# Pacing the Toeplitz loads of the middle chunks in a planned attention-plus-S4 kernel

## The chip, the cores and the metric

The kernel runs on one core of one Trainium2 chip. The metric is the device time of one execution in microseconds (us). A core has five engines that run their own instruction lists side by side and meet only at semaphores: TensorE (PE, matmuls; PEld is its weight load), VectorE (DVE), ScalarE (ACT), GpSimd (POOL) and SyncE (SP, which here only issues DMAs). Matmuls write to PSUM, eight banks of 128 x 512 f32; everything else lies in SBUF or in DRAM. Within one engine's list instructions start in order, so an instruction that waits holds up all that stand behind it on that engine.

## The reference

The output is a gated mix of two branches over a sequence of 2048 tokens with 448 channels, all in bf16:

```python
g = sigmoid((x * gate_w).sum(-1))
a = attention(x)      # 16 query heads of 28, one key and one value head
b = s4(x)             # y = causal convolution of x with K, + x * Dskip
out = g * a + (1 - g) * b
```

The attention is `softmax(q k^T / sqrt(28)) v`, then a 448 x 448 output matrix. The convolution kernel is K[d, l] = Re sum over 256 states n of C[d,n] dB[d,n] exp(l dt[d] A[d,n]); the reference multiplies spectra, which is a causal convolution of length 2048 for each channel.

## The kernel before

**Attention.** Scores are made transposed, in tiles of 128 keys x 512 queries for one head; there are 1024 such tiles. They are taken in turns of three and two, which gives 410 "score sets". For each set PE makes the scores into `psS` (L1318, L1341), ACT takes their exponential into `expT` (L1373), and PE multiplies them with the values into `psB` (L1392). Five PSUM banks hold scores, so the scores of set n (sets are numbered from 0 here) can start when the exponential of set n-2 has read its banks.

**The S4 branch.** The 448 channels go in 14 chunks of 32. For each chunk DVE builds tables of powers (`tables`, L954 to L1004), PE makes the 32 kernels K from them (`kgen`, L1027), DVE copies them to `kstg` (L1039), and POOL writes them to DRAM (`KP_scratch`). From there they come back as Toeplitz matrices: `tload` reads, for each of 8 channels, 128 rows, each the same sequence shifted by one element, into one of the buffers of `T` (three until late in the kernel). One load is four DMAs of 272 KB on SP's queue; 56 loads cover all channels. `conv` then multiplies each Toeplitz block with the input held in `U` (PE, L1094), DVE multiplies the result by 1-g (L1104), PE turns it back (L1115) and DVE adds it to `O` (L1124). `ufill` is another group of DMAs on SP's queue (`U<-T`), which refills `U` for the second half of the channels.

**What sets the order.** Nothing is ordered by hand. Each operation is recorded with an estimated duration, a priority and what it depends on; `Prog.schedule` then plays the engines through in planned time, at each step taking the operation that can start earliest (`key = (r, o.pr, i)`), and writes one list for each engine. The times of this plan exist only while the kernel is built. What is left of them is the order of each list, and the waits that `waits` makes from the dependencies: a wait that an earlier one on the same engine implies is left out. Three things in it matter here.

- A T load takes its turn on SP when its kernels are in DRAM and the last convolution that read its buffer is done.
- After a load the planned time at which its convolution may start is later than the load's planned end by a margin: 56 ns, and `LATE` = 1000 ns more for loads planned before 300000 ns.
- PE's instructions are counted in blocks of 256 (`BLOCK`), and PE may not enter a block in the plan before a set time (`FETCH`) after it entered the one before. Where PE has nothing to do the plan puts in a matmul that has no use (`filler`, L1300).

The first operations of SP's, PE's, DVE's and POOL's lists that a change in the plan moves are thus followed by others: every later choice can fall otherwise. ACT's list has one order.

Of the kernel before, what the change touches and what calls it, by code (L numbers as in the profile page):

```python
# [91 lines left out]
class Prog:  # L92
# [5 lines left out]
    SWITCH = 105.0  # L98
    BLOCK, FIRST, FETCH, IDLE, NEED, QUIET = 256, 158, 4800.0, 3300.0, 0.015, 480000.0
    HALF = (0.0, 0.0, 1.0)  # L100
    PORT = 0.55
    POOL = (7, 5)
    SLACK = {"pe": 500.0, "dve": 300.0}
# [76 lines left out]
    def schedule(self):  # L180
        ops = self.ops
# [17 lines left out]
        order = {e: [] for e in ENG}  # L199
# [5 lines left out]
        npe = 0  # L205
        block = [0.0, 0.0]
        opened = False
        past = []
        self.tot = {}
        self.clock = {e: {} for e in ENG}  # L210
# [4 lines left out]
        while done < n:  # L215
            best = None
            for e in ENG:
                T = free[e]
                for i in ready[e]:
                    o = ops[i]  # L220
                    r = max(rt[i], T)
                    if o.lock is not None:
                        L = min((x for x in locks if x[0] is None), key=lambda x: x[1], default=None)
                        if L is None:
                            continue
                        r = max(r, L[1] + (300.0 if o.pr >= 2 else 0.0))
                    for k in o.comm or ():
                        if k in comm:
                            r = max(r, ops[comm[k]].end)
                    if e == "pe":  # L230
                        j = (npe + o.ni - self.FIRST - 1) // self.BLOCK + 1
                        if j < len(block):
                            r = max(r, block[j])
                            if o.pr >= 1 and block[-1] > r:
                                left = self.FIRST + (len(block) - 2) * self.BLOCK - npe - o.ni
                                r = max(r, block[-1] - left / self.NEED)
                    key = (r, o.pr, i)
                    if best is None or key < best[0]:
                        best = (key, e, i)
            assert best is not None, "scheduler stuck"  # L240
            (r, _, _), e, i = best
            o = ops[i]
            spare = [x for x in locks if x[0] is None and x[1] <= free[e]]
            if e == "pe" and (opened or spare) and r > self.FWIN and self.filler is not None and npe > self.FIRST + self.BLOCK:
                T = free[e]
# [4 lines left out]
                if r - T >= w and busy < self.FLOW * self.FWIN and (j >= len(block) or block[j] <= T):  # L250
                    b = 6 if opened else spare[0][3]
                    o = self.op("pe", lambda x, b=b: self.filler(x, b), self.FILL, rd=["one", "id"], ni=2)
# [7 lines left out]
                    i, r = o.i, T  # L260
                    ready[e].append(i)
            ready[e].remove(i)
            if e == "pe" and o.mode != mode:
                r = max(r, free[e] + self.SWITCH)
# [4 lines left out]
            if e == "pool" and o.slot is None:  # L269
                for d in reversed(order[e]):  # L270
                    if ops[d].slot is None:
                        o.deps[d] = 1
                        break
            order[e].append(i)
            for k in o.comm or ():
                if k in comm:
# [19 lines left out]
            else:  # L296
                ns = o.ns
                if e == "pe" and self.HALF[0] < r < self.HALF[1]:
                    ns *= self.HALF[2]
                free[e] = r + ns  # L300
                end = free[e] + o.lat
                if e == "pool" and o.ns >= 500.0:
                    free["dve"] = max(free["dve"], r) + self.PORT * o.ns
            o.end = end
# [4 lines left out]
            for j in succ[i]:  # L309
                need[j] -= 1  # L310
                x = ops[j]
                if i not in x.deps:
                    t = free[e]
                elif x.eng == e and o.slot is None and e == "pe":
                    t = free[e]
                elif x.eng == e and o.slot is None:
                    t = free[e] + self.SAME[e]
                else:
                    t = end + self.SEM_NS
                    if x.eng == "pe" and x.pr in self.LAZY:  # L320
                        t += self.LAZY[x.pr] if o.slot is None else self.LATE if o.slot[0] == "T" and r < 300000.0 else 0.0
                    if x.pr == 1.45:
                        t += self.FAR
                    elif x.pr >= 2 or x.pr == 1.5:
                        t += self.SLACK.get(x.eng, 0.0)
                rt[j] = max(rt[j], t)
                if need[j] == 0:
                    ready[x.eng].append(j)
# [1159 lines left out]
```

## Time and profile before

| | us |
|---|---|
| median of 3 runs | 499.83 (499.33 to 502.65) |
| the profiled execution, whole | 499.53 |
| its span, first to last instruction | 497.8 |
| ACT busy | 484.2 |
| of it exponentials, 410 of them | 464.5 |
| PE busy | 476.5 |
| DVE busy | 455.1 |
| T loads: median from issue of one DMA to landing | 4.9 |

The profile is one execution. Its page gives busy times of each engine; a chain, which is followed back from the last instruction to what released it; groups of instructions by line; and the DMA issues. L1318 is line 1318 of the kernel before. "PE psS L1094 <- DMA T<-KP_scratch" means that PE stood idle until that DMA landed, and "issue" means that the engine waited for nothing that the profile names. The granted TensorE clock was 1.00 up to 488 us of the span and 0.99 in the rest.

### The profile page before, as it was taken

What the parts mean: (1) busy time and instruction counts of PE and PEld (TensorE: products, weight loads), DVE (VectorE), ACT (ScalarE), POOL (GpSimd) and SP (SyncE); (2) the same over time, 40 slices, a digit from 0 to 9 for tenths busy, and PEclk for the clock granted to TensorE, in tenths of its full rate; (3) what the DMA queues carried; (4) which work ended last, traced back from release to release, by engine and by line L of the source; (5) the groups of instructions that cost most, each with busy time, mean ns of one, the idle gap of its engine ahead of it and who ended that gap; (6) DMA issues with size and microseconds to landing.
All of it is one profiled execution on the core that took longest, in us unless ns stands there. A gap on an engine that the chain in (4) does not pass through costs nothing.

```text
span 497.8 us, 17345 instructions
## 1 busy us (share of the span) xinstructions
PE 476.5 (96%) x7641; PEld 208.2 (42%) x7641; DVE 455.1 (91%) x867; ACT 484.2 (97%) x436; POOL 146.2 (29%) x282
## 2 busy tenths in 40 slices
PE   8899999999999999899999999999999999999997
PEld 6432233343443444444344344444444344344553
DVE  6999999999999999999999999998999999995313
ACT  6999999999999999999999999999999999999995
POOL 2102044234143433224306044520612524251110
PEclk9999999999999999999999999999999999999999
DMA  8997696928529556893953962689793596759742
GB/s 266 324 173 185 118 157 133 261 74 250 152 49 284 166 155 126 247 246 57 288 129 51 285 156 77 184 244 290 176 283 39 144 314 185 212 135 302 234 160 70
DMA packets 152423, 91.86 MB, mean 185 GB/s; under 512 B 84538, under 2 KB 148332, under 8 KB 152348
## 3 DMA queue, kind: packets, MB, share of 16 engines
q1 hardware_dynamic: 143370, 81.21, 61.4%
q0 software_dynamic: 8704, 9.41, 7.6%
q8 instruction: 60, 0.98, 0.8%
q10 hardware_dynamic: 274, 0.14, 0.1%
q14 instruction: 15, 0.12, 0.1%
HBM read 73.61 MB, written 5.23 MB: 158 GB/s over the span
## 4 chain that ended last, share of the span: by engine, by line
ACT 86%; PE 7%; DMA 2%; issue 0%; SPq 0%
ACT expT L1373 85%; DMA T<-KP_scratch 2%; PE psS L1341 1%; PE psS L1318 1%; PE psB L1392 1%; PE psB L1294 1%; PE psS L1231 1%; PE psX L1094 0%; PE psS L1094 0%; SPq L158 0%; PE psB L1300 0%; PE psS L1027 0%; PE psS L873 0%; PE psB L1386 0%; PE psX L1027 0%
## 5 line engine op out<-in xcount | busy, mean ns | idle before, releaser
L1373 ACT ACTIVATE expT<-psS 128x1536 bf16<-128x1536 f32 (+1 forms) x410 | 464.5, 1410 | 2.5 <-PE psS L1341 1.5
L968 DVE TENSOR_TENSOR tab<-tab,mbf 128x512 bf16<-128x512 bf16 (+4 forms) x140 | 139.7, 1002 | 0.0
L1318 PE MATMUL psS<-qT,kT 29*128 29x512 bf16 x684 | 95.7, 385 | 10.7 <-ACT expT L1373 5.5
L1392 PE MATMUL psB<-expT,vaug 128*32 128x512 bf16 x1000 | 99.9, 390 | 0.1
L1341 PE MATMUL psS<-qM,kT 128*128 128x512 bf16 x316 | 95.1, 384 | 1.2 <-ACT expT L1373 0.5
L158 POOL DMA_DIRECT2D KP_scratch<-kstg x104 | 57.4, 559 | 78.1 <-DVE kstg L1039 74.8
L983 DVE TENSOR_TENSOR tab<-tab 128x256 bf16<-128x256 bf16 (+4 forms) x140 | 77.3, 576 | 0.0
L1392 PEld LDWEIGHTS psB<-expT,vaug 128*32 128x32 bf16 x1000 | 25.6, 93 | 73.3 <-issue 70.5
L158 POOL DMA_DIRECT2D qM<-qT x64 | 32.4, 514 | 62.9 <-DVE qT L885 33.0
L1318 PEld LDWEIGHTS psS<-qT,kT 29*128 29x128 bf16 x684 | 23.7, 91 | 64.3 <-ACT expT L1373 51.8
L1300 PE MATMUL psB<-ident,one 128*128 128x512 bf16 x148 | 48.2, 384 | 0.0
L158 POOL DMA_DIRECT2D rdenB<-R_scratch x60 | 31.0, 523 | 48.8 <-DMA R_scratch<-denT 48.7
L1094 PE MATMUL psX<-T,U 128*26 128x128 bf16 (+3 forms) x1728 | 38.6, 221 | 1.2 <-issue 1.0
L1094 PE MATMUL psS<-T,U 128*26 128x128 bf16 (+3 forms) x1536 | 35.6, 221 | 1.1 <-DMA T<-KP_scratch 1.1
L1094 PEld LDWEIGHTS psX<-T,U 128*26 128x26 bf16 (+3 forms) x1728 | 29.6, 105 | 15.0 <-issue 10.0
L158 POOL DMA_DIRECT2D denT<-acc x15 | 10.7, 711 | 85.6 <-DVE acc L1153 72.6
L1094 PEld LDWEIGHTS psS<-T,U 128*26 128x26 bf16 (+3 forms) x1536 | 27.3, 105 | 13.3 <-issue 7.6
L997 DVE TENSOR_TENSOR tab<-tab,tmp 128x1984 bf16<-128x1984 bf16 x28 | 32.4, 1184 | 0.0
L1341 PEld LDWEIGHTS psS<-qM,kT 128*128 128x128 bf16 x316 | 19.0, 97 | 28.5 <-ACT expT L1373 19.5
L991 DVE TENSOR_TENSOR tmp<-tmp,mq 128x64 bf16<-128x64 bf16 (+4 forms) x70 | 25.4, 363 | 0.0
L914 DVE TENSOR_TENSOR msq<-seedz 128x512 f32<-128x512 f32 (+1 forms) x40 | 24.7, 618 | 0.0
L1300 PEld LDWEIGHTS psB<-ident,one 128*128 128x128 bf16 x148 | 13.3, 97 | 22.1 <-issue 14.4
(186 smaller groups left out, 491.2 us busy)
## 6 DMA issues: line engine op xcount, KB each, us to landing
T<-KP_scratch SPq DMA_DIRECT2D x204, 272.0 KB, 4.9
U<-KP_scratch SPq DMA_DIRECT2D x20, 272.0 KB, 5.5
rdenB<-R_scratch POOLq DMA_DIRECT2D x60, 64.0 KB, 4.1
U<-cst SPq DMA_DIRECT2D x1, 3584.0 KB, 25.0
qM<-qT POOLq DMA_DIRECT2D x64, 32.0 KB, 3.3
tab<-in_A_x_dram SPq DMA_DIRECT2D x4, 448.0 KB, 4.7
O<-in_A_x_dram SPq DMA_DIRECT2D x16, 112.0 KB, 4.8
O<-cst SPq DMA_DIRECT2D x1, 1792.0 KB, 9.6
```

The costliest lines, as they stand in the source:

```text
L158: return [e.dma_start(o, i, **kw) for o, i in pairs]
L914: pg.op("dve", lambda e: e.tensor_tensor(m2(msq), z2, z2, ALU.mult), el(2 * n), rd=[kr, ki] + first, wr=["msq"], pr=pr)
L968: mul = lambda e, o, a, b: e.tensor_tensor(o, a, b, ALU.mult)
L983: vo(lambda e, dv=dv, tv=tv, k=k: e.tensor_tensor(dv, dv, tv, ALU.add if k else ALU.subtract), n, [kt[k], kd[k]], [kd[k]], 1.92 if lv else ...
L991: vo(lambda e, w=w, lv=lv: e.tensor_tensor(rho.v(0, P, (32 - 2 * w) * 2, [[64, 32], [2, w], [1, 2]]), rho.v(0, P, (32 - w) * 2, [[64, 32], ...
L997: vo(lambda e, k=k: e.tensor_tensor(tab.v(0, P, FM + k * FP + 2, [[64, 32], [2, 31], [1, 2]]), tab.v(0, P, lm + k * PL + 62, [[64, 32], [- ...
L1094: r = e.matmul(ps.v(32 * j, 32 - m0, 128 * k, [[1, 128]]), self.U.v(0, P, (4 * gi + j) % UA // 2 * 128 + 2 * (2 * m0 + par) + j % 2, [[4, ...
L1300: return e.matmul(t.v(0, P, off, [[1, 512]]), self.one.v(0, P, 2, [[0, P]]), self.ident.v(0, P, 0, [[0, 4], [1, P]]), start=b != 6, stop=b ...
L1318: r = e.matmul(self.psS.v(0, P, 512 * b, [[1, 512]]), kT.v(32 * h, DH + 1, 128 * kt, [[1, 128]]), qT.v(32 * h, DH + 1, 512 * (i % 2), [[1, ...
L1341: return e.matmul(self.psS.v(0, P, 512 * b, [[1, 512]]), kT.v(0, P, 128 * kt, [[1, 128]]), self.qM.v(0, P, (i % 2) * XQ + 512 * h, [[1, 51 ...
L1373: o = pg.op("act", lambda e: e.activation(expT.v(0, P, 512 * es[0], spread(es, n)), self.psS.v(0, P, 512 * bs[0], spread(bs, n)), AF.Exp, ...
L1392: r = e.matmul(self.psB.v(32 * h, 32, 0, [[1, 512]]), vaug.v(0, P, 32 * kt, [[1, 32]]), expT.v(0, P, 512 * ring[t], [[1, 512]]), start=(kt ...
```

## The change

Three edits of the planner, and nothing else. While a T load would start in planned time between 195 and 360 us, it may start no earlier than 5500 ns after the T load before it. For such a load the last exponential that ended by then in the plan becomes a dependency, so the built load waits for ACT's count. And the margin `LATE` of 1000 ns applies to loads that are planned before 360 us instead of 300 us.

```diff
+    GAP, spaced = 5500.0, (195000.0, 360000.0)
...
+        lastT = 0.0
...
+                    if o.slot is not None and o.slot[0] == "T" and self.spaced[0] < r < self.spaced[1]:
+                        r = max(r, lastT + self.GAP)
                     key = (r, o.pr, i)
...
+            if o.slot is not None and o.slot[0] == "T":
+                if self.spaced[0] < r < self.spaced[1]:
+                    for d in reversed(order["act"]):
+                        if ops[d].end <= r:
+                            o.deps[d] = 1
+                            break
+                lastT = r
             order[e].append(i)
...
-                        t += self.LAZY[x.pr] if o.slot is None else self.LATE if o.slot[0] == "T" and r < 300000.0 else 0.0
+                        t += self.LAZY[x.pr] if o.slot is None else self.LATE if o.slot[0] == "T" and r < 360000.0 else 0.0
```

In the built lists ACT's order is unchanged. PE's list is the same up to its 891st of 2364 planned operations (2366 after), DVE's up to the 403rd of 867, POOL's up to the 62nd of 107 and SP's up to the 53rd of 142. Of the 56 T loads, counted from 0, the 22 from 16 to 37 now wait for a score set: for the end of the exponentials of sets 154, 159, 165, 171, 183, 189, 194, 200, 211, 217, 223, 228, 234, 247, 254, 261, 266, 271, 277, 283, 288 and 293. Two fillers are added.

## The prediction

> **What bounds the kernel now.** I read the page's busy times first, then busy times by stretch, then the waits and the chain inside the stretch that the change touches.
>
> ```profile
> PE 476.5 (96%) x7641; PEld 208.2 (42%) x7641; DVE 455.1 (91%) x867; ACT 484.2 (97%) x436; POOL 146.2 (29%) x282
> ```
>
> ACT is the bound: 464.5 us of its 484.2 are the 410 exponentials, so one score set costs 464.5 / 410 = 1.133 us, and no edit here touches an exponential. What can be won is ACT's idle time. By stretch (the columns are the stretch, its length, and the busy us and counts of PE, PEld, DVE, ACT, POOL, then clock, DMA share and GB/s):
>
> ```profile
> 0.00:20.00 20.00, 16.57 (x191) 11.33 (x192) 15.48 (x33) 14.91 (x19) 3.26 (x19) 1.00 0.96 293
> 20.00:195.00 175.00, 169.33 (x2185) 66.36 (x2181) 173.69 (x346) 174.21 (x157) 53.76 (x97) 1.00 0.70 169
> 195.00:360.00 165.00, 158.97 (x2818) 69.85 (x2810) 161.50 (x307) 163.29 (x146) 54.92 (x102) 1.00 0.71 183
> 360.00:455.00 95.00, 92.66 (x1600) 40.64 (x1601) 93.09 (x161) 95.00 (x86) 31.08 (x58) 1.00 0.70 200
> 488.00:497.80 9.80, 6.93 (x87) 3.36 (x87) 3.06 (x8) 3.82 (x5) 0.00 (x0) 0.99 0.33 89
> ```
>
> From 195 to 360 us ACT is idle for 165.00 - 163.29 = 1.71 us; before that for 0.79 from 20 us on, after it until 488 for nothing. The rest of its 13.6 idle us lies in the first 20 us and the last 9.8, which the edits do not reach. So 1.71 us is the most that the middle can give. DVE is nearly as full there: 3.50 us idle of 165, 1.91 of the next 95. The chain from 195 to 360 us (start, length, what) shows where the 1.71 are:
>
> ```profile
> 194.19 13.57 ACT expT L1373 x12
> ...
> 208.20 0.34 PE psX L1094 x15
> 208.55 0.96 issue
> 209.51 0.49 PE psX L1094 x21
> ...
> 211.80 114.46 ACT expT L1373 x101
> ...
> 331.86 7.70 DMA T<-KP_scratch
> 339.56 0.04 issue
> 339.60 0.25 PE psS L1094 x4
> ...
> 341.89 18.19 ACT expT L1373 x16
> ```
>
> There are two stalls. At 208.55 PE stands 0.96 us in the middle of a convolution, on nothing that the profile names; ACT then loses 0.56 us at 210.58 and 0.20 at 211.80. Near 339 PE waits for load 32; the waits put its size and ACT's loss as follows (total us, times, longest):
>
> ```profile
> PE psS L1094 <- DMA T<-KP_scratch: 1.1, 1, 1.1
> PE psX L1094 <- issue: 1.0, 1, 1.0
> ACT expT L1373 <- PE psS L1341: 1.3, 2, 0.7
> ```
>
> ACT's three idle gaps there (0.08 at 336.28, 0.75 at 340.74, 0.13 at 341.89) make 0.96.
>
> **The late load.** In the trace loads 29 to 34 were issued at 313.7, 319.1, 324.2, 329.9, 333.2 and 336.8. Where the records have all four landings, a load took 6.4 to 9.6 us from its first issue to its last landing: 6.4 for load 15, with nothing near it, 9.0 and 9.3 for loads 30 and 33. Load 32 had until its convolution 8.6 us or so (329.9 to 338.5, where PE went idle) and needed 9.7. In the new order it waits for the end of set 266 and its convolution stands behind the scores of set 277, which start when set 275 ends: 9 sets, 9 x 1.133 = 10.2 us, and some 0.4 for those scores. Counted likewise, loads 16 to 37 get 7 to 23 sets; only loads 30 and 36 get 7 (7.9 + 0.4 = 8.3 us), eight get 8 (9.5 us). That is above what a load takes with little beside it (6.4 to 7.9), and below the worst (9.6). I take it that this stall goes: **-0.96**. From both sides: 0 if spaced loads still take 9.6, -0.96 if not; nearest is load 15.
>
> **The stall at 208.55 stays.** PE's list is unchanged up to its 891st operation, and the stall lies in operations 879 to 887. Loads 16 and 17 now also wait for sets 154 and 159, which ended at 201.0 and 206.4; they were issued at 200.8 and 205.7 because PE then freed their buffers. So they move by 0.2 and 0.7 us. What PE waits for: the records of the DMA queue for instructions (q8 on the page: 60 transfers of 16 KB for 2 x 7641 PE instructions, about 255 in each) show one that began at 207.03 and ended at 208.18; PE went on 1.33 us later. By the count of PE's instructions the block in front of it began at 204.0. The transfer began when load 16's last packets did (207.2). The next one began at 212.51, when load 17's last packets did. With no T load under way such transfers began within 0.8 us of their block. So a code block waits behind a T load under way, whether or not another follows. Worth of this edit at this place: 0, and the next block, due at 214.97 with its transfer done at 213.46, could be up to 0.5 late now that load 17 comes 0.7 later.
>
> [...]
>
> **The added waits.** 22 waits on SP, each at the head of four DMAs. Behind each stand the rest of that load, the next loads, and pieces of the refill of `U`. The refill pieces are wanted much later: the first were issued at 185.2 and read from 320.1 on, the last at 378.8 and from 470.5 on. The next load is meant to wait. SP has the time: one DMA issue takes 0.6 us (median 615 ns), so a load takes 2.5. Cost 0 beside the leads above. The margin held to 360 us moves convolutions behind other work in PE's list; PE's work is the same but for two fillers (0.215 us each), which stand where PE would idle. Cost 0.
>
> **The rest of the order.** DVE's list changes from entry 403 on. Its work is the same; at the late load it waited 1.28 us (340.94) and 0.45 (347.62), and should gain those. Blocks of PE code can fall worse, which I bound by 0 and two stalls of 0.76 and put at one half of one: **+0.4**, and +0.1 for load 17's shift.
>
> The sum: 499.53 (the profiled execution; its span is 497.8, and 1.7 lies outside) - 0.96 + 0.4 + 0.1 = **499.1**. This is 0.7 under the median of the three runs, 499.83, whose lowest is 499.33. About 1%, 5 us here, is what a measurement of this kernel can tell from no change, so my forecast is "no change": 498.4 to 499.8.
>
> **Rival A, slower: DVE falls behind.** The planner put `kgen` on PE right behind the tables: in the trace the DVE instruction that it waits for ended 0.06 to 3.4 us before `kgen` starts, 0.94 us for the last chunk (453.52 to 454.46). DVE has no gap to catch up in (3.6 us of waits in all from 195 to 455). If the new list has DVE wait at convolutions that come later than planned, every us beyond 0.94 holds PE at `kgen`, and with it scores and ACT, one for one; load 52, behind the last tables, landed only 0.9 us before its convolution. One such wait costs what the rows at 210.06 (1.14) and 340.94 (1.28) cost, 1.2. The 22 loads feed 11 convolutions with two DVE operations each; with five to nine of the 22 waiting it is 498.6 + 6.0 - 0.9 = 503.7 to 498.6 + 10.8 - 0.9 = 508.5. It decides from the first us of DVE waits over today's. For it: DVE's full rows. Against: in the old order only two of its convolution operations waited over 1 us.
>
> **Rival B: code blocks take the stall's place.** By instruction counts PE passes 256 instructions in as few as four sets (4.5 us). The new order does so from sets 163, 212, 262 and 304, and at 304 and at 274 (5.2 sets) a load's packets begin as the block does. Such a block's transfer starts up to 3.7 us late, and with 1.0 and 1.33 needs 6.1: 0.2 to 1.5 us short. Two to four stalls of 0.76: 500.1 to 501.6.
>
> **Rival C: it does not do what it says.** The waits are met before the other waits of the same loads, as with load 16, or loads 5.5 us apart still take 9: 499.5. For it: load 30 came 5.4 us after load 29 and took 9.0. Against: from load 18 on the score set is the later wait for most.
>
> **Chances.** Forecast 0.42, A 0.28, B 0.16, C 0.10; 0.04 for over 1% faster, which needs 5 us where 1.71 are to be had. Three quarters of A lies over 504.8: slower 0.21. Same: 0.42 + 0.16 + 0.10 + 0.07 = 0.75. Range: 498.0 leaves out the fast case, 505.5 some 0.16 of A.
>
> **What would show it.** Right: no wait of PE for a T load from 320 to 345; T loads issued 5 us and more apart from load 18 on; the "issue" wait at 209 still there; ACT idle from 195 to 360 near 1 us. B: more "issue" waits of PE near 1 us there. A: `kgen` (L1027 before) waiting for DVE, and more DVE waits at the multiplication behind a convolution. The forecast is wrong if ACT loses time past 360 us, where it loses none now.

## The result and the profile after

| us | before | after |
|---|---|---|
| median of 21 runs each | 500.66 (498.82 to 503.99) | 502.86 (500.37 to 505.87) |
| ratio of after to before | | 1.0049, 95% interval 1.0032 to 1.0066 |
| the profiled execution, whole | 499.53 | 502.29 |
| its span | 497.8 | 500.4 |
| ACT idle, 195 to 488 us of the span | 1.71 | 3.95 |
| ACT idle in all the rest of the span | 11.9 | 11.7 |
| ACT busy | 484.2 | 484.8 |

The changed kernel is 0.5% slower. That is inside the 1% that the forecast called "no change" and inside its range, 498.0 to 505.5, whose upper part stood there for rival A, which did not come. But it is outside the 498.4 to 499.8 that the forecast gave for itself, and on the other side of the kernel before: 499.1 was forecast, 0.7 us under the median shown then.

The page of the changed kernel, its busy times:

```profile
PE 462.2 (92%) x7560; PEld 207.3 (41%) x7643; DVE 455.0 (91%) x867; ACT 484.8 (97%) x436; POOL 145.7 (29%) x282
```

ACT is still the bound. Some 83 matmul records of PE are missing here (7560 beside 7643 weight loads), so PE's busy time is not compared with the 476.5 of before. Busy time by stretch, with the columns as shown for before:

```profile
195.00:360.00 165.00, 152.98 (x2773) 69.23 (x2800) 161.65 (x310) 163.00 (x146) 54.68 (x102) 1.00 0.74 183
360.00:455.00 95.00, 89.01 (x1588) 40.15 (x1603) 92.83 (x158) 94.22 (x85) 29.96 (x56) 1.00 0.72 205
455.00:488.00 33.00, 29.91 (x753) 16.24 (x755) 6.98 (x14) 31.83 (x29) 4.23 (x9) 1.00 0.58 178
```

ACT, the fourth pair, is idle for 2.00 us in the first stretch (1.71 before), 0.78 in the second and 1.17 in the third, where it was never idle before. These 2.24 us more are nearly all of the 2.6 by which the span grew; 0.5 is ACT's own busy time. Of what PE and ACT waited for from 195 to 488 us, the lines that matter here (total us, times, longest):

```profile
ACT expT L1384 <- PE psS L1329: 3.8, 4, 1.3
PE psX L1105 <- DMA T<-KP_scratch: 2.4, 2, 1.5
PE psS L1105 <- issue: 1.1, 1, 1.1
PE psS L1105 <- DMA T<-KP_scratch: 0.9, 1, 0.9
```

Before, PE waited 1.3 us for T loads there; now it is 3.3. And the chain in the same stretch (start, length, what; L1384, L1329 and L1105 are the lines L1373, L1318 and L1094 of before):

```profile
214.55 0.33 SPq L159
...
217.22 7.15 DMA T<-KP_scratch
...
224.41 1.03 PE psX L1105 x60
...
317.88 7.32 DMA T<-KP_scratch
...
325.25 0.42 PE psX L1105 x16
...
374.40 5.68 DMA T<-KP_scratch
380.12 0.48 PE psS L1105 x20
...
475.84 1.11 issue
476.94 0.58 PE psS L1105 x27
```

Load 32, for which PE stood at 339 us before, is on time. In its place PE stands for load 18 (1.51 us at 222.9, of which ACT loses 1.32), load 30 (0.91 at 324.3; ACT 0.68) and load 38 (0.86 at 372.4; ACT 0.67) with load 39 behind it (0.15; ACT 0.07), and at 475.84 it stands 1.11 us on nothing named (ACT 1.08). The last packets of these loads came 9.0, 8.5, 9.9 and 11.7 us after their first issue.

Load 18 shows what SP's list has to do with it. That list, as the trace has it, first before, then after, by start, length and number of DMAs (`x4` of `T` is one load; `U<-T` are the refill pieces):

```profile
206.99 5.61 SPq L158 DMA_DIRECT2D T<-KP_scratch  x6
213.16 0.71 SPq L158 DMA_DIRECT2D U<-T  x1
214.28 5.16 SPq L158 DMA_DIRECT2D T<-KP_scratch  x4
219.48 4.97 SPq L158 DMA_DIRECT2D U<-T  x4
```

```profile
207.62 1.27 SPq L159 DMA_DIRECT2D T<-KP_scratch  x2
211.43 2.76 SPq L159 DMA_DIRECT2D U<-T  x2
214.29 3.55 SPq L159 DMA_DIRECT2D T<-KP_scratch  x4
217.88 1.35 SPq L159 DMA_DIRECT2D U<-T  x2
220.00 3.69 SPq L159 DMA_DIRECT2D T<-KP_scratch  x4
```

Before, the first six are the end of load 17 and load 18, issued at 210.1; the refill starts behind it. After, two refill pieces stand ahead of load 18, which is issued at 214.3.

The queue is not all of these 4.2 us. The load's own wait, for set 165, ended at 213.1: 3.0 us are the distance that the change asks for, and its convolution comes 2.9 us later as well (PE stands for it from 222.9; before, PE began it at 220.0). 1.2 us are the queue. The transfer then took 9.0 us to its last packet in place of 6.9. At the other two late loads no refill piece stands directly ahead. Load 30 was issued 0.1 us after its set 254 had ended; three pieces stand behind it, of which the second took 5.5 us to issue. Load 38 has no set wait, follows load 37 by 2.7 us (3.7 before), and has one piece behind it.

### The profile page after: what moved, and what is told of

Read it like the earlier page. It is cut to its first block, busy times and chain, and to the rows that moved or that the text cites. A ratio compares the mean times of both kernels' runs of the same rounds, so it can differ in the third digit from the quotient of the medians.

```text
span 500.4 us, 17277 instructions
## 1 busy us (share of the span) xinstructions
PE 462.2 (92%) x7560; PEld 207.3 (41%) x7643; DVE 455.0 (91%) x867; ACT 484.8 (97%) x436; POOL 145.7 (29%) x282
## 4 chain that ended last, share of the span: by engine, by line
ACT 77%; PE 11%; DMA 4%; SPq 1%; issue 1%
ACT expT L1384 77%; DMA T<-KP_scratch 4%; PE psS L1329 2%; PE psS L1352 2%; PE psB L1403 1%; SPq L159 1%; PE psS L1105 1%; PE psX L1038 1%; PE psX L1105 1%; PE psS L1242 1%; PE psB L1305 1%; PE psX L1144 0%; PE psB L1311 0%; PE psS L1038 0%; PE psS L884 0%
## 5 line engine op out<-in xcount | busy, mean ns | idle before, releaser
L1384 ACT ACTIVATE expT<-psS 128x1536 bf16<-128x1536 f32 (+1 forms) x410 | 465.0, 1379 | 4.7 <-PE psS L1329 4.0
L1329 PE MATMUL psS<-qT,kT 29*128 29x512 bf16 x684 | 95.7, 385 | 12.4 <-ACT expT L1384 7.1
L1352 PE MATMUL psS<-qM,kT 128*128 128x512 bf16 x242 | 78.5, 382 | 12.2 <-issue 8.5
L1329 PEld LDWEIGHTS psS<-qT,kT 29*128 29x128 bf16 x684 | 23.7, 91 | 65.6 <-ACT expT L1384 52.2
L1311 PE MATMUL psB<-ident,one 128*128 128x512 bf16 x150 | 49.8, 384 | 0.0
L1105 PE MATMUL psS<-T,U 128*32 128x128 bf16 x1984 | 45.5, 221 | 2.5 <-issue 1.4
L1105 PEld LDWEIGHTS psS<-T,U 128*32 128x32 bf16 x1984 | 34.8, 105 | 19.3 <-issue 11.8
L1105 PE MATMUL psX<-T,U 128*26 128x128 bf16 (+3 forms) x1280 | 28.2, 221 | 2.7 <-DMA T<-KP_scratch 2.4
L1105 PEld LDWEIGHTS psX<-T,U 128*26 128x26 bf16 (+3 forms) x1280 | 21.8, 105 | 12.3 <-issue 6.0
L1038 PE MATMUL psX<-tab 128*64 128x128 bf16 x608 | 25.1, 223 | 0.0
```

Source lines behind the costliest of these rows:

```text
L1038: r = e.matmul(G.v(64 * u, 64, 128 * k, [[1, 128]]), tab.v(0, P, lo + comp * PL + cg * 64 + u, [[2, 64]]), tab.v(0, P, fo, [[64, 2], [mo - ...
L1105: r = e.matmul(ps.v(32 * j, 32 - m0, 128 * k, [[1, 128]]), self.U.v(0, P, (4 * gi + j) % UA // 2 * 128 + 2 * (2 * m0 + par) + j % 2, [[4, ...
L1311: return e.matmul(t.v(0, P, off, [[1, 512]]), self.one.v(0, P, 2, [[0, P]]), self.ident.v(0, P, 0, [[0, 4], [1, P]]), start=b != 6, stop=b ...
L1329: r = e.matmul(self.psS.v(0, P, 512 * b, [[1, 512]]), kT.v(32 * h, DH + 1, 128 * kt, [[1, 128]]), qT.v(32 * h, DH + 1, 512 * (i % 2), [[1, ...
L1352: return e.matmul(self.psS.v(0, P, 512 * b, [[1, 512]]), kT.v(0, P, 128 * kt, [[1, 128]]), self.qM.v(0, P, (i % 2) * XQ + 512 * h, [[1, 51 ...
L1384: o = pg.op("act", lambda e: e.activation(expT.v(0, P, 512 * es[0], spread(es, n)), self.psS.v(0, P, 512 * bs[0], spread(bs, n)), AF.Exp, ...
```

## The experiments

Each kernel was timed beside runs of the kernel before on the same chip. The theories, in the order in which they came up: the set waits take the loads' lead (1, later W); the new order of PE and DVE costs by itself (2, later O); late loads (L); PE code held up behind T loads (C); the place of the refill pieces among the loads on SP (R). The theories of late loads and of the order were both open after the trace of the changed kernel, since the plan moved every engine's list at once.

### The parts of the change, one at a time

**order_only**: the new lists, without the waits.

```diff
-                if self.spaced[0] < r < self.spaced[1]:
-                    for d in reversed(order["act"]):
-                        ...
                 lastT = r
```

> The lists of the changed kernel on every engine, but the 22 waits on score sets left out of the built loads. Theory 1 (the waits take the lead that a load had: a load that waits is late, since refill pieces and other transfers make it take up to 9 us): loads 18 and 30 start up to 4 us earlier and PE no longer waits for them (1.51 and 0.91 us in the changed kernel); load 38, which has no such wait, can still be late. ACT gains back 1.3 + 0.7, so 0.4 us over the kernel before instead of 2.4. Theory 2 (the new order of PE and DVE costs, whatever the loads wait for): as slow as the changed kernel, 2.4 us over the kernel before.

**waits_only**: the lists of before, the waits at its own planned starts.

```diff
-                        r = max(r, lastT + self.GAP)
+                        r = max(r, lastT + 0.0)
...
-  ... self.LATE if o.slot[0] == "T" and r < 360000.0 else 0.0
+  ... self.LATE if o.slot[0] == "T" and r < 300000.0 else 0.0
```

> The lists of the kernel before on every engine, with waits on score sets added to its middle loads: each for the last exponential that the plan has finished when the load starts there, no 5500 ns between loads. Theory 1 (waits alone can make loads late): these waits stand where the loads started in the plan of before, so they hold a load back by 1 us at most; one more late load at worst, 0 to 1 us over the kernel before. Theory 2 (order): no difference from the kernel before, within 0.5 us.

**gap_only**: distance and waits, the margin as before.

```diff
-  ... self.LATE if o.slot[0] == "T" and r < 360000.0 else 0.0
+  ... self.LATE if o.slot[0] == "T" and r < 300000.0 else 0.0
```

> The distance of 5500 ns with its waits, the margin of 1000 ns still ending at 300 us. Lists as in the changed kernel up to PE's operation 1498 (near 310 us). Theory 1: load 18 late as in the changed kernel (1.3 us of ACT), loads after 300 us later still, their convolutions being planned 1 us closer: 3 us or more over the kernel before. Theory 2: between the kernel before and the changed one, at 1 to 2.4 us over.

**margin_only**: the kernel before with the margin to 360 us alone.

```diff
-  ... self.LATE if o.slot[0] == "T" and r < 300000.0 else 0.0
+  ... self.LATE if o.slot[0] == "T" and r < 360000.0 else 0.0
```

> No distance and no waits on score sets; only the margin of 1000 ns held to 360 us. Lists as before up to PE's operation 1467 (near 305 us). Theory 1: load 32's wait of 1.06 us goes and nothing is put in its place: 0.5 to 1 us under the kernel before. Theory 2: any new order costs, 0 to 1.5 us over.

| | median us | ratio to before, 95% interval |
|---|---|---|
| before, 35 runs | 500.37 | |
| order_only | 502.47 | 1.0040 (1.0011 to 1.0069) |
| waits_only | 500.47 | 1.0009 (0.9988 to 1.0031) |
| gap_only | 501.02 | 1.0017 (0.9994 to 1.0039) |
| margin_only | 500.28 | 1.0000 (0.9977 to 1.0024) |

On the old lists the waits cost nothing that can be told, and taking them out of the new ones leaves nearly the whole loss (502.47 here; 502.86 with them): theory 1 falls as the main cause, though up to 1 us for the waits is not excluded by these intervals, and the profile of waits_only has loads late by 0.57 us at 335 and 0.73 at 371 that before has not. The margin alone costs nothing. It gains nothing that can be told either, though in its profile PE waits for no T load from 195 to 488 us: ACT is idle for 1.75 us there, all of it behind stands on nothing named. What costs is the new lists, and in gap_only, whose PE list is the changed kernel's up to its 1498th operation and so past load 18, that load is late too: PE stood 1.84 us for it. The time of gap_only, 0.7 us over before, is under what either theory forecast, and is not told from before.

### What of it goes through the T loads

**before_nowait and after_nowait**: the lists of before and after; convolutions read a constant tile in place of the loaded one and wait for no load, while every load still runs.

```diff
-     tbuf.v(0, P, to + j * TC + 32 * (13 - 2 * m0 - par), [[1, 128]]),
+     self.kT.v(0, P, 256 * j + 32 * (13 - 2 * m0 - par), [[1, 128]]),
```

> The lists of the kernel before; the convolutions read a constant in place of the loaded Toeplitz blocks, so PE waits for no T load, while every load is still made in full. (The convolution's result is left wrong.) Late loads cost the kernel before 0.96 us of ACT in its profile. Theory L (late loads make the difference between the two kernels): 0.5 to 1 us under the kernel before. Theory C (PE's code blocks, which wait behind T loads, and the half clock that follows a long stand make it): the same gain here, since it is the loads' only place in this kernel; 209 us still shows a stand of 0.7 to 1.2 us on nothing named.

> The same edit on the changed kernel: its lists, its waits on score sets, all loads in full, no wait of PE for a T load. (The convolution's result is left wrong.) In its profile late loads cost 2.7 us of ACT. Theory L: all of the difference goes, this kernel and before_nowait are equal within 0.5 us. Theory C: 1 us or more over before_nowait remains, and half of the executions still show a mean clock under 0.9985.

**before_small and after_small**: the same lists and waits; after the first use of each buffer a T load moves 32 rows of 64 bytes in each DMA.

```diff
-  ap=[[4 * rs, 32], [TC, 8], [1, TC]]
+  ap=[[4 * rs, 32], [TC, n], [1, m]]      # n, m = (8, TC) if first else (1, 32)
```

> The lists and waits of the kernel before, but after the first load into each buffer a T load moves 32 rows of 64 bytes by each of its DMAs in place of 272 KB (the convolution's result is left wrong): no load can be late and no code block can stand behind one. Both theories: no stall at 209 or 340, ACT idle from 195 to 488 under 0.5 us, 1 to 2 us under the kernel before.

> The same on the changed kernel. Both theories L and C: equal to before_small within 0.5 us, since every loss of the new order comes by way of the T loads' transfers. A third theory (the new order of PE and DVE itself is slower, with no transfer in it): 1 to 2.4 us over before_small.

| | median us | ratio to before (499.91, 35 runs) |
|---|---|---|
| before_nowait | 498.97 | 0.9985 (0.9958 to 1.0013) |
| after_nowait | 500.40 | 0.9992 (0.9961 to 1.0023) |
| before_small | 497.48 | 0.9944 (0.9919 to 0.9969) |
| after_small | 498.28 | 0.9947 (0.9922 to 0.9971) |

With small loads the two orders are the same by their ratios (0.9944 and 0.9947), and neither profile has a gap on ACT between 195 and 488 us: what separates the kernels goes in the main through the transfers of the T loads. Their medians are 0.8 us apart, which twelve executions of each do not tell from zero (means 0.6 apart, -0.5 to 1.7). With full loads for which nobody waits, ACT still lost 0.58 and 0.97 us to stands of PE on nothing named at 327 and 475 us in after_nowait, and 0.64 to one at 345 in before_nowait. This pair's intervals are too wide to say how much of the difference is late loads.

### Three loads, and earlier waits

**after_again**: the changed kernel a second time. **waits_early**: the same lists, each set wait on a set that ends 3.4 us earlier. **after_three**: the changed kernel with three loads small.

```diff
-                        if ops[d].end <= r:
+                        if ops[d].end <= r - 3400.0:          # waits_early
...
+            n, m = (1, 32) if gi in (18, 30, 38) else (8, TC)  # after_three, in tload
```

> The changed kernel once more, as the measure for the two beside it and for a second profile. **If the stands recur with the order**, PE waits again for T load 18 near 224 us (1.5 us in the first profile), for load 30 near 325 us (0.9) and for load 38 near 373 us (0.9), and stands on nothing named for 0.8 to 1.2 us near 209 or 476 us; ratio to before 1.003 to 1.007. **If they are chance**, other loads are late, or none, and the sum of ACT's gaps between 195 and 488 us is well away from the 3.9 us of the first profile.

> The lists of the changed kernel on every engine, and the same 22 waits, but each on a score set that ends at least 3.4 us ahead of the planned start of its load, not just ahead of it. **Theory W (the waits take the lead of load 18)**: in the first profile of the changed kernel load 18 was issued at 214.3 us against 210.1 before and came 1.5 us late; the full-clock runs of the kernel with the new order and without waits were 1.1 us below the changed one. With earlier waits load 18 is issued by 212 us, the gap of 1.3 us on ACT near 226 us goes, and the time is 0.8 to 1.3 us below the changed kernel in this call. **Theory O (the order, not the waits)**: the time stays within 0.5 us of the changed kernel.

> The changed kernel, in which T loads 18, 30 and 38 alone move 32 rows of 64 bytes in each DMA in place of 256 rows of 1088 bytes, so that most of these three tiles keeps what an earlier load put there and the output is not the reference's; everything else, the waits too, is unchanged. The three are the late ones of the first profile. **Theory L (the late loads)**: all three stands go, 1.32 + 0.68 + 0.67 = 2.7 us on ACT, and the time falls by 2.0 to 2.7 us below the changed kernel, to a ratio of 0.999 to 1.001 to before. **Theory C (code held behind T loads)**: the loads that are left whole hold the code as before, and stands on nothing named near 209, 328 or 476 us take part of the place: the time falls by 0.5 to 1.5 us.

| | median us | ratio to before (500.00, 30 runs) |
|---|---|---|
| after_again | 503.83 | 1.0060 (1.0038 to 1.0082) |
| waits_early | 503.33 | 1.0054 (1.0028 to 1.0081) |
| after_three | 500.06 | 0.9995 (0.9971 to 1.0018) |

Shrinking three of 56 loads takes away the whole difference: 3.8 us between after_again and after_three, and the intervals are apart. It takes the traffic of these loads away too, and the kernel before with three loads small was not run, so this is not the price of their lateness alone. The stretches of after_three:

```profile
195.00:360.00 165.00, 154.93 (x2795) 69.95 (x2823) 163.80 (x317) 165.00 (x148) 54.86 (x102) 1.00 0.70 172
360.00:455.00 95.00, 89.66 (x1600) 40.88 (x1616) 91.14 (x152) 94.94 (x86) 31.01 (x58) 1.00 0.70 199
```

ACT has no idle time at all in the stretch where it lost 2.00 us in after and 2.33 in after_again. From 195 to 488 us it was idle for 1.23 us, against 4.63 in after_again. The gain is more than the 2.7 us that theory L took from the first profile: the stands on nothing named at 209 and 328 us (1.57 and 0.84 in after_again) are missing too; the one at 478 us (1.21) stayed.

By the records of the instruction queue (q8, 60 transfers of 16 KB in a profile) these stands are read as waits for code. In all twenty profiles PE stood 46 times for over 0.3 us on nothing named between 195 and 488 us. 44 of these stands ended 1.24 to 1.57 us after the end of such a transfer, where its 60 transfers are some 8 us apart; the other two lie in stretches where the granted clock was 0.50. At 475.84 us in the first profile of the changed kernel the transfer ended at 475.67 and PE went on at 476.95. What made a transfer late is not shown: in after_again the one for 327 us began at 325.1, 2.5 us after the last packet of load 30.

So there are two ways in which ACT loses time. Its idle time from 195 to 488 us, put down to the last stand of PE ahead of each gap:

| kernel | behind late T loads, us | behind stands on nothing named, and the rest, us |
|---|---|---|
| before | 1.0 | 0.8 |
| after | 2.7 | 1.2 |
| after_again | 1.6 | 3.0 |
| waits_early | 2.1 | 2.2 |
| after_three | 0 | 1.2 |

In the first profile late loads are the larger part, in the second late code. Theory C is not refuted by after_three, since both ways close when loads are small (ACT idle for 0.00 us from 195 to 488 in before_small and after_small).

after_again was late for loads 18 (0.62), 38 (0.81) and 39 (0.72) again, so these are no accident of one execution; for load 30 PE did not wait. And theory W falls a second time: with earlier waits load 18 was issued at 214.3 us all the same, straight behind the two refill pieces, and came 1.80 us late.

### The place of the refill pieces on SP

**order_behind**: order_only with the refill pieces that stood between T loads 17 and 19, 29 and 31, 36 and 39 moved behind loads 19, 31 and 39. **before_refill_front**: the lists of before, load 18 moved behind the first two pieces. **order_refill_small**: order_only, the pieces in place but nearly empty. **before_behind**: the lists of before, pieces moved behind loads 19, 32 and 39. PE, DVE, ACT and POOL keep their lists in all four.

```diff
+        for a, b in ((17, 19), (29, 31), (36, 39)):        # order_behind; before_behind has (29, 32)
+            T = [x for x in seq if x[1].slot is not None and x[1].slot[0] == "T"]
+            i, j = seq.index(T[a]), seq.index(T[b])
+            uf = [x for x in seq[i:j] if x[1].slot is not None and x[1].slot.startswith("uf")]
+            seq = [x for x in seq[:j + 1] if x not in uf] + uf + seq[j + 1:]
...
+        seq = seq[:i] + seq[i + 1:j] + uf + [T[18]] + ...   # before_refill_front: uf, two pieces; i, j: load 18, first piece
...
-        lst = [(self.U.v(0, P, c * 2048, [[128, 16], [1, 32]]), ...
+        lst = [(self.U.v(0, P, c * 2048, [[128, 1], [1, 32]]), ...   # order_refill_small
```

> The new lists without set waits, with one difference, on SP alone: refill pieces of U that stood between T loads 17 and 19, 29 and 31, 36 and 39 stand behind loads 19, 31 and 39. The lists of PE, DVE, ACT and POOL are unchanged. **Theory R (the pieces' place)**: load 18 is issued near 210 us in place of 214 to 215, is there by 218, and PE waits for none of loads 18, 30, 38; without the pieces ahead the time falls by the 1.7 us (full clock) to 2.5 us (all runs) that these lists stood above before: 499.5 to 501.0 us, a ratio of 0.999 to 1.001. **Theory O (the order of the compute engines)**: the time stays at 501.5 us or above, a ratio of 1.003 to 1.005.

> The lists of before, with one difference, on SP alone: T load 18 stands behind the first two refill pieces of U, as in the new lists, not ahead of them. **Theory R**: load 18 is issued at 214 to 215.5 us and is there at 222.5 to 224.5, where PE wanted it at 220.0: a stand of PE of 2.5 to 4.5 us, of which 1.5 to 4 us reach ACT, and a half-clock stretch behind it in most runs: 502 to 504.5 us, a ratio of 1.003 to 1.009. **Theory O**: load 18 is as late, but the old order of PE has other work to give; below 500.8 us, a ratio under 1.002.

> The new lists without set waits and unchanged on every engine; each refill piece of U keeps its place but copies 1 of 16 rows of 64 bytes for each partition, so that U keeps old data for most of the second half and the output is not the reference's. **Theory S (sharing the DMA engines)**: load 18 is still issued at 214 to 215 us, but takes 7 us in place of 9 and is there by 222, load 38 takes 7.5 in place of 9 to 10; PE waits for neither, and the time falls by 1 to 2.5 us to a ratio of 0.998 to 1.001. **Theory P (place on the queue alone)**: the loads take the same 9 to 10 us, the waits stay, ratio 1.003 to 1.005.

> The lists of before, with one difference, on SP alone: refill pieces that stood between T loads 17 and 19, 29 and 32, 36 and 39 stand behind loads 19, 32 and 39. **Theory R**: load 19 takes 7 us in place of 10.9, load 32 is there a little sooner and the stand of 1.06 us at 340 us shrinks to under 0.5; the time falls by 0 to 1 us, a ratio of 0.998 to 1.000. **If the pieces only hit other loads**, one of loads 20 to 23, 33 to 36 or 40 to 42 becomes late, and the ratio is 1.000 to 1.003.

| | median us | ratio to before (500.01, 29 runs) |
|---|---|---|
| order_behind | 500.61 | 1.0019 (0.9990 to 1.0048) |
| before_refill_front | 507.38 | 1.0128 (1.0089 to 1.0167) |
| order_refill_small | 500.55 | 1.0012 (0.9984 to 1.0039) |
| before_behind | 499.56 | 0.9995 (0.9975 to 1.0015) |

(One of the six executions of before_refill_front took 962.0 us, for a reason that its record does not show; the ratio leaves it out.)

before_refill_front changes nothing but the place of one load among the DMAs of one queue, and the kernel before loses 1.3%. Its chain:

```profile
208.59 1.59 issue
...
215.89 2.19 SPq L158
...
220.30 4.90 DMA T<-KP_scratch
...
225.25 0.41 PE psX L1108 x8
```

Load 18 was issued at 218.1 and PE stood 3.36 us for it, in a kernel whose order of PE and DVE is the old one. ACT was idle for 8.33 us from 195 to 360, against 1.71. At this place theory O is refuted. The cost is above what R expected: of ACT's 6.6 us more, 3.46 are the wait for load 18 itself, and 1.6 each fell behind it and around the stand of 209 us, where the clock went to 0.50 (last section).

Put together, load 18 in the kernels so far whose T loads are full and waited for (us of the span; "came" is its last packet; PE's first matmul on it):

| kernel | refill pieces ahead | issued | came | PE starts | PE stood for it |
|---|---|---|---|---|---|
| before | 0 | 210.1 | 217.0 | 220.0 | 0 |
| waits_only | 0 | 209.7 | 217.1 | | 0 |
| margin_only | 0 | 210.6 | 217.6 | 220.5 | 0 |
| before_behind | 0 | 210.2 | 217.4 | | 0 |
| order_behind | 0 | 211.0 | 218.3 | | 0 |
| after | 2 | 214.3 | 223.3 | 224.4 | 1.51 |
| after_again | 2 | 214.1 | 223.1 | 224.4 | 0.62 |
| waits_early | 2 | 214.3 | 223.2 | 225.8 | 1.80 |
| gap_only | 2 | 214.9 | 224.0 | 225.1 | 1.84 |
| order_only | 2 | 215.2 | 223.9 | 225.3 | 0 |
| order_refill_small | 2, nearly empty | 213.5 | 221.9 | 223.7 | 0.28 |
| before_refill_front | 2 | 218.1 | 224.5 | 225.2 | 3.36 |

With the pieces ahead it is issued some 4 us later, and where the new lists have it there it also takes longer, 8.7 to 9.1 against 6.9 to 7.5. The queue alone is enough for these 4 us: in order_only, which has no set wait, and in waits_early, whose set wait was over by 210.5, the first piece itself waits for PE (until 213.5 and 212.5), and the load, issued at 215.2 and 214.3, stands behind it. In after the set wait would have held the load until 213.1 without any piece. There is other company than the pieces: at 215.8 to 218.9 us POOL issues one DMA of 448 KB (`xT<-XS_scratch`) in every kernel of the table, old order and new. Before, load 18 was in by then and load 19 met it (10.9 us, with time to spare). With nearly empty pieces load 18 still took 8.4. So at load 18 the place is the larger part and sharing the engines with the pieces the smaller, as P has it; load 38 took 7.5 with nearly empty pieces and 9.9, 9.8 and 9.1 with full ones (after, after_again, order_only), as S has it. The time went as S forecast: with the pieces nearly empty in their old place these lists take 500.55 us, and 500.61 with the pieces moved, where P forecast no gain. A nearly empty piece is issued faster as well (the second one ahead of load 18 in 0.9 us, against 2.1 in after), so this run does not part the place from the size. order_only shows no wait for load 18 because PE had been held by a stand of 1.24 us at 209.8 and by the clock behind it (0.53 from 210.8 to 214.4), and came as late as the load.

order_behind moved load 18 ahead of the pieces, and PE waited for none of 18, 30 and 38; but five pieces now stood ahead of load 32, which came 1.70 us late.

### Side by side

The intervals of order_only and order_behind overlap. So the new lists without waits once more (**order_again**), and beside them the same with the pieces behind load 32 as well (**order_behind32**).

```diff
-        for a, b in ((17, 19), (29, 31), (36, 39)):
+        for a, b in ((17, 19), (29, 32), (36, 39)):
```

> The new lists without set waits once more, as the measure for the run beside it: 502 to 503 us, a ratio of 1.003 to 1.006, with load 18 issued at 214 to 215.5 us behind two refill pieces.

> As the new lists without set waits but with the refill pieces behind loads 19, 32 and 39, so that load 32, which stood behind five pieces in the first move and came 1.7 us late, has none ahead of it. **Theory R (the pieces' place)**: load 18 at 210 to 211 us, no wait of PE for a T load of over 0.3 us between 195 and 455 us; 499.5 to 500.8 us, 1.5 us or more below the kernel beside it. **Theory O (the order of the compute engines)**: within 0.7 us of the kernel beside it.

| | median us | ratio to before (500.61, 23 runs) |
|---|---|---|
| order_again | 502.87 | 1.0036 (1.0008 to 1.0065) |
| order_behind32 | 501.01 | 1.0007 (0.9989 to 1.0026) |

SP's list around load 18 in order_again and then in order_behind32, the columns as above:

```profile
214.00 1.67 SPq L159 DMA_DIRECT2D U<-T  x2
215.71 3.59 SPq L159 DMA_DIRECT2D T<-KP_scratch  x4
```

```profile
207.90 8.58 SPq L159 DMA_DIRECT2D T<-KP_scratch  x9
216.53 8.28 SPq L159 DMA_DIRECT2D U<-T  x3
```

The same instructions of PE, DVE, ACT and POOL in the same order are 1.9 us faster when eleven refill pieces stand behind these loads, not between them: of the 2.3 us that these lists stand above before, 0.4 is left. The intervals of the two ratios still overlap; the executions of the two kernels compared with each other give 1.8 us, 0.2 to 3.4. What PE waited for in order_behind32, the lines as above:

```profile
PE psX L1113 <- DMA T<-KP_scratch: 1.2, 2, 1.0
PE psS L1113 <- issue: 1.1, 1, 1.1
PE psS L1113 <- DMA T<-KP_scratch: 1.0, 2, 0.9
```

The waits expected to be under 0.3 us were not: load 37 came 1.03 late (363 us) and load 38 0.86 (372 us). 37 is planned just inside 360 us and 38, past the end of the spacing, follows it by 2.7 us. R forecast the gain of 1.5 us or more, which came, and 499.5 to 500.8 us, where 501.01 was measured; what it said of these two loads did not hold.

Nor does the gain lie where R had it. ACT's idle time from 195 to 488 us, put down as above:

| kernel | behind late T loads, us | behind stands on nothing named, and the rest, us |
|---|---|---|
| order_only | 0.4 | 3.4 |
| order_again | 0.6 | 3.7 |
| order_behind | 1.5 | 3.0 |
| order_behind32 | 1.6 | 1.2 |
| order_refill_small | 0.1 | 0.4 |

In one profile of each, order_behind32 loses 1.0 us more behind late loads than order_again and 2.5 us less behind late code and the low clock. That the place of the pieces on SP makes the difference is shown by changing nothing else. That it does so by late T loads is shown for load 18 by before_refill_front, and not for the whole.

### Looking for a kernel below both

**margin_u2000** was margin_only with 2 us more planned for two early loads of the input, since two profiles had shown DVE late behind one (2.8 us at 59 us).

```diff
-            self.late.append(pg.dma(lst, (1024, 896), f"u{k}", wr=[("ust", k)], pr=0.3).i)
+            self.late.append(pg.dma(lst, (1024, 896), f"u{k}", wr=[("ust", k)], pr=0.3, extra=2000).i)
```

> The order of before with the planner's margin to 360 us, and 2 us more planned for the two O loads in the first 60 us, behind which DVE came late in two profiles (2.8 us at 59 us, PE 2.5 us behind it, and granted clock 0.5 from 59 to 63 us). It looks for a kernel below both. **If the early stand is a late O load that the plan can be warned of**, no wait of DVE for O is over 1 us, there is no half clock before 100 us, and the time is 0.5 to 2 us below before (ratio 0.996 to 0.999). **If the plan pays for it**, its later order gives the 2 us back, and the ratio is 0.999 to 1.004.

504.68 us, 1.0083 (1.0053 to 1.0113): the early stand was gone from its profile, but the whole plan behind it was another one, with a T load 1.11 us late at 367 us and stands of 1.40 and 1.43 us on nothing named at 453 and 483 us. The other candidate is **before_behind** above: no late load at all, ACT idle for 0.86 us from 195 to 488, all of it at the stand of 209 us, and 0.9995 (0.9975 to 1.0015). No kernel here that keeps the output is measurably below the kernel before.

## Why the prediction was wrong

**What bounds the kernel**: right. ACT, and only its idle time moved, but for 0.5 us.

**The late load, -0.96**: the part about load 32 held. In the changed profiles PE does not wait for it. What failed is the rule behind the term, that 8 sets (9.5 us) of lead are enough, and with it that no other load becomes late. This is the first step that failed. Loads 18, 30 and 38 (38 lies past the 22 that were counted) had 8.6, 8.8 and 9.6 us from first issue until PE stood, and PE went on 10.1, 9.7 and 10.5 us after the issue. The count of sets itself was good: for load 18 it gave 8 sets, 9.5 us, from the end of set 165 at 213.1, and PE came at 222.9. But the load was taken to go out with its wait and alone. Load 18 lost 1.2 us of its lead in SP's queue, and its company on the DMA engines (9.0 us to the last packet) was not the little that load 15 had (6.4). For load 30 the count gave 8.3 us, under the 9.0 that this load had taken in the trace of before, and it was let pass. In place of -0.96 this term is -0.96 + 1.32 + 0.68 + 0.67 + 0.07 = +1.8, and +0.7 in the second profile, where late loads cost 1.64. Spacing did not shorten the loads by much: first issue to last packet of loads 16 to 37 is 7.63 us on average before and 7.23 after, since what lengthens them is not the load before alone.

**The added waits, 0**: right as far as the runs can tell; taking them out or making them earlier moved 0.4 to 1.0 us, less than the intervals resolve. At load 18 that is so because the queue holds the load as long without its wait. But it was this step that named the refill pieces, and only as something that may stand behind a load. It did not look at which now stand ahead of one.

**The rest of the order, +0.4**: this is the second step that failed. It went through DVE's list and the blocks of PE's code, and left out SP's, the one queue on which the change acts. The built list showed it before any run: one piece behind load 18 in the old order, two ahead of it in the new one. The reason lies in the planner: a load that may not be planned for 5.5 us leaves SP free, and the plan takes the next thing that can start. order_behind32 gives back 1.9 us of 2.3 (1.8, 0.2 to 3.4, by the direct comparison) by undoing this alone, without set waits; the changed kernel with its waits and with the pieces moved was not run. The size was off for code too: late code and what follows it cost ACT 1.2 us in the first profile and 3.0 in the second, against 0.8 before. The shift of load 17, +0.1, did not matter.

**The stall at 208.55 stays**: right as a rule, not in the first profile, where DVE waited 0.40 us at 209.2 and ACT lost nothing. It is 1.57 us in after_again and 0.7 to 1.6 in nine of the other kernels, but 0.5 or less in after_three, order_behind32, order_refill_small and the kernels whose convolutions wait for no load or a small one. It comes in some executions and lists and not in others. Where it comes it ends 1.24 to 1.56 us after its code transfer does, as the prediction read it (1.33); what makes that transfer late in one execution and not in another was not found.

**Rival A** fell. In the changed profile no stand of PE between 195 and 488 us ended with a DVE instruction.

**Rival B** was part of it. At 475.84 PE stood 1.11 us, where before has no stand. Near 476 us (481 in order_only) it recurs in all nine profiles with the new lists, full refill pieces and full loads (0.5 to 1.8 us; in after_three only three loads are small), and is missing in after_small. But waits_only, with the lists of before, and margin_only have one near there too (0.5 and 1.2), so it is not owed to the new order alone. That it is a block of code which came late is read from the records of the transfers (the one ahead of it ended at 475.67, PE went on at 476.95); that a T load held the block up was not tested by itself.

**Rival C** named the right fact, loads 5.5 us apart that still take 9, but had them in its old place, where they cost what they cost before. The direction was missed because no rival had a load that comes later through SP's order.

The line that would make the forecast wrong was drawn at the right place: ACT lost 1.95 us past 360 us.

## What to carry to other kernels

Before a transfer is delayed in an ordered queue, list what moves ahead of it there. Here two refill pieces filled the slot that load 18 left, and in order_only the first of them waited for PE until 213.5 us and load 18 behind it went out at 215.2, against 210.1 before. Count a transfer's lead from where it can be issued (load 18 lost 1.2 us of it in the queue), and its length in the company that it will have at the new time, which includes transfers of other engines: 10.9 us for load 19 of before, with POOL's 448 KB under way, against 6.4 for load 15 alone. When several engines' lists move at once, put one list back by itself; here the list of one queue was enough for most of a loss that looked like one of the whole order, as far as 1.8 us with an interval of 0.2 to 3.4 can say.

## What the runs showed of the hardware that was not expected

**A stand of PE can cost twice.** The stretches of before_refill_front around its two stands; the third column from the right is the granted clock:

```profile
208.50:210.50 2.00, 0.41 (x28) 0.32 (x20) 0.46 (x1) 1.56 (x2) 0.00 (x0) 1.00 0.84 289
210.50:211.00 0.50, 0.49 (x14) 0.11 (x2) 0.27 (x1) 0.00 (x0) 0.00 (x0) 1.00 1.08 387
211.00:214.00 3.00, 2.79 (x55) 1.45 (x57) 3.00 (x4) 1.54 (x2) 0.61 (x2) 0.50 0.19 63
...
225.20:226.50 1.30, 1.25 (x15) 0.40 (x19) 1.30 (x4) 0.26 (x1) 0.00 (x0) 0.50 1.01 316
226.50:229.50 3.00, 2.67 (x64) 1.59 (x57) 3.00 (x10) 2.22 (x2) 0.00 (x0) 0.50 0.91 191
```

The stand of 1.59 us ends at 210.18; from 211.0 us the clock is 0.50 for 3.4 us, and again from 224.7, within the stand of 3.36, for 6.8. ACT lost 1.26 us directly at the first stand and 1.14 right behind it. order_only has the same after a stand of 1.24 us (0.53 from 210.8 to 214.4 us). But stands of 1.51 us (after), 1.57 (after_again), 1.80 (waits_early) and 1.84 (gap_only) were not followed by it (the clock is 1.00 from 195 to 360 us in all four), so the length of a stand alone does not decide. What else decides was not found.

It may be a part of this result. Executions whose mean granted clock is under 0.9985 were 38 of the 152 of the kernel before that ran beside the experiments (median 501.81 us, the others 499.71), 18 of 33 of the changed kernel (504.06 and 502.39), 16 of 24 of its lists without waits and 7 of 24 of those with the refill behind. If the low clock is what makes these executions longer, then 0.30 more of them at 1.7 to 2.1 us each are 0.5 to 0.6 us of the changed kernel's loss, by estimate; longer stands in the same executions could be part of it.

**An issue can take as long as a load.** SP's issue of one DMA takes 0.6 us (the median of before). With other transfers under way it took 2.1 to 6.9 us in the cases that follow. Two refill pieces in before_behind, straight behind loads 18 and 19:

```profile
217.85 7.56 SPq L158 DMA_DIRECT2D U<-T  x2
```

The second of the two took 6.9 us to issue, as long as load 18 of before took from first issue to last packet, from 218.5 to 225.4, while POOL's 448 KB DMA (issued at 217.6) and load 19 (last packet at 224.4) were under way; load 18 was in by then. In after, the second piece ahead of load 18 took 2.1 us (212.1 to 214.2), 1.5 us more than the median, and load 18 waited that out too; the four DMAs of load 39 took 7.20 us in after and 2.55 before. So part of what a queue costs is in the issue itself, which the sum of the prediction had at 2.5 us for a load throughout. What holds an issue was not tested.
